# First batch's q and k: rotation products added by accumulating f32 transposes, one v scale, a rewritten order

## The chip, the core and the metric

The kernel runs on one core of a Trainium2 chip. The metric is the device time of one execution in microseconds (us). Five engines work side by side: PE (matrix multiply, with its weight loads, PEld), DVE (vector), ACT (scalar, activation functions), POOL (general) and SP, which here only issues DMAs. Each runs its own list of instructions in order and waits on semaphores for the others.

## What is computed

Attention with rotated q and k over 4 batches, 8 heads, 576 positions and 64 channels, then a feed-forward layer over all 2304 rows:

```python
x1, x2 = x[..., :half], x[..., half:]           # half = 32, x is q or k
rot = concat([x1*cos - x2*sin, x1*sin + x2*cos], -1)
scores = rot_q @ rot_k.T / sqrt(64)
attn = exp(scores - max(scores)); attn = attn / (attn.sum(-1) + 1e-9)
x = attn @ v                                    # to (2304, 512)
h = x @ w_in                                    # w_in 512 x 2048
out = (h * sigmoid(h)) @ w_out                  # w_out 2048 x 512
```

## The kernel before, in words

Heads are taken in pairs p = 0 to 3. A unit u is half a batch (two chunks of 128 rows); what is left of each batch, 64 rows, forms one more unit, "rem". A slot is one head of a pair with one chunk of rows: scores (task `S`), row maximum, exponential, and the transposed probabilities. The feed-forward layer goes by steps (u, i) with i = 0 to 7 over eight pieces of w_in and w_out: `m1` is 24 matmuls (L1200), then tanh, gating and a split into two f16 parts on ACT, DVE and POOL, then two `m2` tasks of 6 matmuls each (L1257). Weights and most operands are split into a high and a low f16 part, which needs a scale: a mean square, spread over the partitions by a matmul with ones, and cut to a power of two by three tiny DVE operations (`add_scale`, L299 to L323, tasks sc0, sc1, sc2).

The first unit is handled apart, since nothing can overlap it yet. Its q and k stay in f32 (`add_qk_first`, L432): the load puts head j and four rows side by side; r0 (L458) writes x, its halves swapped, times sin into a tile `rt`; r1 (L462) multiplies x by cos in place; r2 (L465) adds the two. Each handles 576 columns in one instruction on DVE or POOL. `tr` (L471 to L478) then makes 10 transposes on PE into a PSUM tile, and `ev` copies it to SBUF. The slots of unit 0 (`add_slot_first`) use f32 matmuls (L915) and f32 transposes (L928).

The first batch's v is split as well (`add_v`, L612): a Gram matrix on PE (`trace`, L343) and its diagonal on DVE give the sum of squares of each pair; each pair has its own ones matmul (L647) and its own scale. `add_v_scale` (L690) forms one more scale over the maximum of the four, by a transpose, a maximum and another matmul (L695 to L701).

A raw weight piece is loaded into a place of the weight tiles or of a ring (three parts a, b, c), truncated (wT, wC, wX: L766, L773, L779), its mean square is found by Gram matmuls on PE (L351) or by a Square on ACT (L807), and it is split (whi, wlo). While batch 0 is raw, its q, k and v lie in places that later weights want.

What runs when is written out by hand. `add` records a task with its engines, its dependencies and buffers; the string `ORDER` (L38) lists all 2557 tasks by number, each with its engine (s = SP, t = PE, a = ACT, d = DVE, p = POOL), and the loop at the end of the kernel issues them in this order. An engine's list is thus the order of its letters in the string, and nothing reorders it.

Of the kernel before, what the change touches and what calls it, by code (L numbers as in the profile page):

```python
# [8 lines left out]
F32 = mybir.dt.float32  # L9
# [29 lines left out]
498s 500p 499a 4s 501d 1s 5d 2s 6d 7p 10p 11d 12d 26s 3s 8t 27d 28d 0d 13t 29p 494s 32d 9a 14d 495a 496a 15s 504t 689t  # L39
497d 502a 690d 33p 505d 34p 699t 691a 700d 16t 30t 17d 18t 31a 503d 506t 59s 19d 20d 507d 508d 21d 48s 692t 49p 50d  # L40
509d 81s 60t 704t 51d 514s 61d 62t 63d 64d 701a 702t 82t 693a 54d 512a 510p 511d 83d 22a 52t 65d 513d 703a 53a 35t 36a
55d 66a 84t 85d 516a 694t 24d 695d 696a 37s 38t 39d 86d 70s 76d 518s 56p 520a 71d 87d 68d 515a 88a 705d 40t 706a 57t
72p 519a 41d 697t 698a 42d 90d 707t 709t 522s 523a 58a 521d 524p 92t 525d 528t 25s 517d 526a 77p 527d 93d 540s 708d
529d 541a 73d 710d 43d 78d 44d 94t 530t 531d 532d 99s 533d 711a 46d 74t 75a 538p 101s 102a 103a 539p 1901d 536d 712t
110p 713a 560s 714t 95d 715d 719t 720d 588s 724t 716a 717t 590p 721a 537p 718a 116d 104t 562p 725d 726a 722t 723d 79t
727t 542a 544s 105d 80a 96d 728a 106d 678d 561a 107d 1902t 546a 97d 729t 739t 740d 741a 730d 731a 534p 734t 735d 589a
1903d 736a 535d 1904t 742t 743a 100s 117p 732t 733a 1908d 564s 565a 1905d 591d 545a 737t 738a 563d 47s 749t 750d 751a
744t 1911t 752t 745d 566a 547d 746a 111p 112p 113a 543d 1906p 753a 584s 585a 550t 747t 567d 1907p 118d 548t 551d 568t
549d 569d 580s 570a 571d 552t 553d 119p 748a 132s 554d 586p 572t 555d 558p 587d 581a 582a 573d 754t 755d 756a 759t
760d 1915d 574d 1909t 764t 765d 575d 1910a 761a 1912d 108d 583d 757t 758a 762t 766a 1922d 763a 556p 592a 1916t 594t  # L50
559p 595d 767t 593d 768a 1917d 596t 597d 598d 1923t 769t 557d 785t 69s 578a 599d 770d 602p 604a 1913p 1918t 786d 771a
# [141 lines left out]
def rope_attention_silu_ffn(  # L193
# [99 lines left out]
    th_v = [sm(NPC) for b in range(B)]  # L293
    alpha, alpha_g, c_st = sm(NPC), sm(NPC), sm(NPC)
    r_max, rem_os = sm(1), sm(2)
    bits_r = [sm(2) for _ in range(4)]
    bits_n = [0]

    def add_scale(key, src, inv, s, deps, bufs, it, last=True):  # L299
# [1072 lines left out]
```

## Time and profile before

| | us |
|---|---|
| median of 3 runs | 638.02 (636.32 to 639.64) |
| the profiled execution | 635.93 |
| its span, first to last instruction | 634.1 |
| PE busy in the span | 595.7 (94%) |
| DVE, ACT, POOL busy | 473.4 (75%), 393.1 (62%), 325.4 (51%) |
| mean granted clock of PE, as a share of full speed | 0.976 |

Busy time is the union of an engine's instructions. A row of a timeline gives start, length, engine, line, operation, output and inputs; "idle before" names what ended the wait. The chain of waits is found from the last instruction backwards, at each step to what released it. The granted clock is 1.00 at 2.4 GHz and 0.50 at 1.2 GHz; a window's value is the mean over it.

### The profile page before, as it was taken

To read this page: it belongs to the slowest core of one execution; us is meant where nothing else is said; L and a number is where in the kernel's file an instruction comes from. 1 tells how busy PE (TensorE), PEld (TensorE's weight loads), DVE (VectorE), ACT (ScalarE), POOL (GpSimd) and SP (SyncE) were. 2 spreads that over 40 slices of the span, in tenths; PEclk is the share of its full clock that TensorE was granted. 3 is DMA by queue.
4 is the path that set the end of the run, shared out by engine and by line. 5 is a ranking of instruction groups with operands and counts; after the bars stand their busy time and mean duration, and the time that the engine had idled before them with its cause. 6 is when DMAs were issued, how large, how long until landed. Compare 5 with 4: busy or idle time off the path is not lost.

```text
span 634.1 us, 12527 instructions
## 1 busy us (share of the span) xinstructions
PE 595.7 (94%) x4476; PEld 392.9 (62%) x4476; DVE 473.4 (75%) x1088; ACT 393.1 (62%) x816; POOL 325.4 (51%) x286
## 2 busy tenths in 40 slices
PE   0989887999999999999999999999999999999997
PEld 0657654566566656756666666666666676666663
DVE  2796877899999899978878998988799775322211
ACT  1576867998798776868777677666644633112322
POOL 2448244856566646554766256366754665221231
PEclk9975979989999999999999999999999999999999
DMA  6895506998989998989995897897965746200201
GB/s 177 258 318 212 158 2 156 230 242 173 178 177 176 171 181 158 150 170 172 173 208 122 137 173 150 162 193 141 155 111 96 129 80 124 51 1 1 51 2 33
DMA packets 210670, 91.17 MB, mean 144 GB/s; under 512 B 188464, under 2 KB 194352, under 8 KB 210608
## 3 DMA queue, kind: packets, MB, share of 16 engines
q1 hardware_dynamic: 209840, 89.36, 68.2%
q10 hardware_dynamic: 768, 1.02, 0.7%
q8 instruction: 35, 0.57, 0.4%
q14 instruction: 27, 0.22, 0.1%
HBM read 36.73 MB, written 4.72 MB: 65 GB/s over the span
## 4 chain that ended last, share of the span: by engine, by line
PE 79%; DVE 7%; DMA 6%; ACT 4%; SPq 2%; issue 1%; DVEq 0%; ACTq 0%
PE m L1200 28%; PE m L1257 26%; PE s L1043 7%; PE pv L1145 7%; PE s L915 2%; PE s L1034 2%; DMA Tq<-n 1%; DVE pn L338 1%; PE s L928 1%; PE s L1049 1%; DMA w_in<-in_v_dram 1%; DMA w_out<-in_moe_w_out_dram 1%; PE pv L982 1%; DMA w_out<-in_v_dram 1%; PE s L351 1%
## 5 line engine op out<-in xcount | busy, mean ns | idle before, releaser
L1200 PEld LDWEIGHTS <-w_in 128*128 128x128 f16 x1728 | 168.1, 99 | 33.9 <-issue 3.6
L1200 PE MATMUL m<-xh,w_in 128*128 128x256 f16 x1024 | 179.9, 274 | 0.3 <-DVE g L1216 0.3
L1257 PE MATMUL m<-w_out,gh 128*128 128x512 f16 x576 | 171.6, 379 | 0.0
L1200 PE MATMUL m<-xl,w_in 128*128 128x256 f16 x512 | 140.4, 274 | 0.0
L1077 ACT ACTIVATE e<-s,small 128x576 f32<-128x576 f32 x128 | 97.9, 765 | 62.2 <-DVE s L1059 18.4
L1257 PE MATMUL m<-w_out,gl 128*128 128x512 f16 x288 | 109.2, 379 | 0.2 <-POOL gl L341 0.2
L1216 DVE SCALAR_TENSOR_TENSOR g<-g,m 128x512 f32<-128x512 f32 x72 | 49.1, 682 | 70.0 <-ACT g L1212 39.4
L338 DVE SCALAR_TENSOR_TENSOR pn<-e,small,pn 128x576 f16<-128x576 f32 x94 | 85.9, 918 | 4.2 <-ACT pn L332 3.1
L1257 PEld LDWEIGHTS <-gh 128*128 128x128 f16 x576 | 51.8, 99 | 56.0 <-issue 5.1
L1212 ACT ACTIVATE g<-m,small 128x512 f32<-128x512 f32 x64 | 43.6, 682 | 51.4 <-PE m L1200 44.0
L1043 PE MATMUL s<-Tk,Tq 128*128 128x512 f16 (+1 forms) x384 | 60.8, 286 | 2.1 <-ACT e L1077 2.1
L332 ACT ACTIVATE pn<-e,small 128x576 f16<-128x576 f32 x69 | 52.4, 767 | 12.9 <-DVE small L1091 9.5
L1059 DVE TENSOR_SCALAR_CACHE_REDUCE s<-s,small 128x576 f32<-128x576 f32 x67 | 54.3, 816 | 2.0 <-PE s L1043 1.3
L326 POOL TENSOR_SCALAR g<-g,small 128x512 f32<-128x512 f32 x27 | 21.9, 811 | 64.8 <-ACT gh L332 30.7
L1145 PE MATMUL pv<-pt,vh 128*64 128x320 f16 (+1 forms) x504 | 54.1, 290 | 0.0
L326 POOL TENSOR_SCALAR e<-e,small 128x576 f32<-128x576 f32 x34 | 31.0, 911 | 39.6 <-ACT pn L332 16.9
L1257 PEld LDWEIGHTS <-gl 128*128 128x128 f16 x288 | 28.2, 98 | 34.6 <-POOL gl L341 0.7
L326 POOL TENSOR_SCALAR pn<-e,small 128x576 f16<-128x576 f32 x31 | 26.5, 854 | 41.5 <-DVE small L1091 31.5
L341 POOL TENSOR_TENSOR pn<-e,pn 128x576 f16<-128x576 f32 x34 | 45.4, 1335 | 2.8
L1043 PEld LDWEIGHTS <-Tq 128*128 128x128 f16 x384 | 28.3, 100 | 27.5 <-issue 7.0
L332 ACT ACTIVATE gh<-g,small 128x512 f16<-128x512 f32 x40 | 28.7, 718 | 16.5 <-DVE g L1216 11.9
L338 DVE SCALAR_TENSOR_TENSOR gl<-g,small,gh 128x512 f16<-128x512 f32 x45 | 35.7, 793 | 4.0 <-ACT gh L332 2.7
(212 smaller groups left out, 1057.8 us busy)
## 6 DMA issues: line engine op xcount, KB each, us to landing
w_out<-in_moe_w_out_dram SPq DMA_DIRECT2D x4, 1024.0 KB, 5.7
w_in<-in_moe_w_in_dram SPq DMA_DIRECT2D x4, 1024.0 KB, 6.5
out_dram<-ob SPq DMA_DIRECT2D x28, 128.0 KB, 2.4
io<-in_q_dram SPq DMA_DIRECT2D x12, 288.0 KB, 3.2
io<-in_k_dram SPq DMA_DIRECT2D x12, 288.0 KB, 3.7
io<-in_v_dram SPq DMA_DIRECT2D x12, 288.0 KB, 4.2
io<-in_v_dram SPq DMA_DIRECT2D x13, 256.0 KB, 4.5
ring<-in_moe_w_in_dram SPq DMA_DIRECT2D x3, 1024.0 KB, 5.8
```

The source lines that it names most:

```text
L326: e.tensor_scalar(out=out, in0=in0, scalar1=s1, scalar2=s2, op0=ALU.mult, op1=ALU.bypass if s2 is None else ALU.mult)
L332: act.activation(hi, src, AF.Copy, scale=s)
L338: dve.scalar_tensor_tensor(out=lo, in0=src, scalar=s, in1=hi, op0=ALU.mult, op1=ALU.subtract)
L341: e.tensor_tensor(out=lo, in0=src, in1=hi, op=ALU.subtract)
L1043: pe.matmul(o, tq[:, j, 2 * c:2 * c + 2, :], kt[:, r0:r1, js], start=(n == 0), stop=(n == 1))
L1059: dve.tensor_scalar(out=t, in0=t, scalar1=cc[1], scalar2=None, op0=ALU.mult, op1=ALU.min, accum_out=m_of(1, 2),)
L1077: act.activation(buf("e", i), buf("s", i)[:, 0:S], AF.Exp, bias=m_of(1, 2), scale=-1.0 if fused[i] else cc[0], accum_out=m_of(2, 3),)
L1145: pe.matmul(o[64 * j:64 * j + 64, 0:m], vt[part][:, j, s, :], pt[:, a, j, 0:m], start=(z == 0), stop=(z == len(steps) - 1),)
L1200: pe.matmul(t[:, c, 0:n], w[:, wz, kk, fs], xx[:, kk, 0:n], start=(kk == 0 and x == 0), stop=(kk == KD - 1 and x == 2),)
L1212: act.activation(g[:, :, 0:n], t[:, :, 0:n], AF.Tanh, scale=th_v[units[u][0]][:, i:i + 1])
L1216: dve.scalar_tensor_tensor(out=g, in0=g, scalar=1.0, in1=t, op0=ALU.add, op1=ALU.mult)
L1257: pe.matmul(o, gs[gz][:, c, ts], w[:, wz, c], start=(first and c == 0 and x == 0), stop=(last and c == 1 and x == 2),)
```

## The change

For the first batch's q and k the sum r2 is gone. Each of the two products is now written to a tile of its own, sin into `rt` and cos into a tile `n` (which later batches use too; two buffers), with the two heads of a pair interleaved, so that a product is three instructions (256, 256 and 64 columns) in place of one of 576. x itself is no longer written. The transposes became pairs of matmuls in transpose mode, the cos product first and the sin product second into the same PSUM columns, the second accumulating: 12 for a tile in place of 10. The cos product no longer depends on the sin product.

The first batch's v has one scale for hi and lo of all four pairs: five small matmuls with ones into one PSUM row, one run of sc0, sc1, sc2 over 5 columns. The four ones matmuls and their scales, the transpose, the maximum and its matmul are gone; every `vhi` of batch 0 now depends on the Gram diagonals of all four pairs.

The mean square of a weight may be taken on ACT where the piece came in two loads, too. ORDER is new throughout: 2531 tasks.

```diff
...
-498s 500p 499a 4s 501d 1s 5d 2s 6d 7p 10p 11d 12d 26s 3s 8t 27d 28d 0d 13t 29p 494s 32d 9a 14d 495a 496a 15s 504t 689t
+3s 472s 474p 473a 2s 1s 4s 9p 10p 475d 478a 468s 469a 11t 0d 6d 12d 5p 7t 8a 470d 471d 476a 663t 664d 673t 665a 479d
...
-    bits_r = [sm(2) for _ in range(4)]
+    bits_r = [sm(5) for _ in range(4)]
...
-            def r0(e, x4=x4, nm=nm):
-                eng[e].tensor_tensor(out=buf("rt", 0, p, nm), in0=x4()[:, :, ::-1, :], in1=sin_t, op=ALU.mult)
-
-            def r1(e, x4=x4):
-                cs = cos_t[:, :, None, :].to_broadcast([128, NR, 2, 32])
-                eng[e].tensor_tensor(out=x4(), in0=x4(), in1=cs, op=ALU.mult)
-
-            def r2(e, x4=x4, nm=nm):
-                eng[e].tensor_tensor(out=x4(), in0=x4(), in1=buf("rt", 0, p, nm), op=ALU.add)
-
-            n = add("rope", key + (nm, 0), "dp", r0, [("qld",) + key, ("sin0",)], xb + [rt], it)
-            n = add("rope", key + (nm, 1), "dp", r1, [n, ("cos0",)], xb + [rt], it)
-            n = add("rope", key + (nm, 2), "dp", r2, [n], xb + [rt], it)
-
-            def tr(i=i, nm=nm):
+            def turned(which, nm=nm):
+                if which:
+                    return buf("rt", 0, p, nm).rearrange("p r u d -> p (r u d)")
+                return buf("n", 0, p, nm).rearrange("p r d -> p (r d)").bitcast(F32)
+
+            def product(e, which, x4, tab, turned):
+                o = turned(which)
+                for j in range(2):
+                    dst = o[:, 0:512].rearrange("p (a j u d) -> p j a u d", a=4, j=2, u=2)[:, j]
+                    rs = slice(4 * j, 4 * j + 4)
+                    eng[e].tensor_tensor(out=dst, in0=x4[:, rs], in1=tab[:, rs], op=ALU.mult)
+                dst = o[:, 512:576].rearrange("p (u d) -> p u d", u=2)
+                eng[e].tensor_tensor(out=dst, in0=x4[:, 8], in1=tab[:, 8], op=ALU.mult)
+
+            def r0(e, x4=x4, turned=turned):
+                product(e, 1, x4()[:, :, ::-1, :], sin_t, turned)
+
+            def r1(e, x4=x4, turned=turned):
+                product(e, 0, x4(), cos_t[:, :, None, :].to_broadcast([128, NR, 2, 32]), turned)
+
+            def tr(nm=nm, turned=turned):
                 t = buf(turn[nm], "q", p, nm)
                 for a in range(4):
-                    o = t[:, 128 * a:128 * a + 128]
-                    pe.transpose(o, x()[:, i, a + 3:a + 5, :], id_t)
-                    pe.transpose(o[0:64], x()[:, i, a, :], id_t)
-                pe.transpose(t[:, 512:576], x()[64:128, i, 7:9, :], id_t[64:128, 64:128])
-                pe.transpose(t[0:64, 512:640], x()[:, i, 8, :], id_t)
+                    for z in range(2):
+                        pe.matmul(
+                            t[:, 128 * a:128 * a + 128], turned(z)[:, 128 * a:128 * a + 128], id_t,
+                            is_transpose=True, start=(z == 0), stop=(z == 1),
+                        )
...
+
+            nb = bk("n", 0, p, nm)
+            n = add("rope", key + (nm, 0), "dp", r0, [("qld",) + key, ("sin0",)], xb + [rt], it)
+            y = add("rope", key + (nm, 1), "dp", r1, [("qld",) + key, ("cos0",)], xb + [nb], it)
...
+            n = add("qP", key + (nm,), "t", tr, [n, y, ("ident",)], [nb, rt, sb], it)
             add("qE", key + (nm,), "ad", ev, [n], [sb, bk("T" + nm, 0, p)], it)
...
+            for z in ("inv", "s"):
+                vn[b][z], vn[b][z + "_p"] = vn[b][z + "5"][:, NP:NP + 1], vn[b][z + "5"][:, 0:NP]
...
             y = add("vtr", key, "t", gram, [("vld",) + key], [pb] + fb, it)
-            n = add("vsq", key, "d", diag, [y, ("ident",), ("ones",)], [pb], it)
+            add("vsq", key, "d", diag, [y, ("ident",), ("ones",)], [pb], it)
+            n_sc = ("sc2", "vs", 0)
         else:
             n = add("vsq", key, "a", sq, [("vld",) + key], fb + vb, it)
-        n = add("vmm", key, "t", mm, [n, ("ones",)], [pb], it)
-        n_sc = add_scale(("v",) + key, lambda: ps()[:, 256:257], st["inv"], st["s"], [n], [pb], it)
+            n = add("vmm", key, "t", mm, [n, ("ones",)], [pb], it)
+            n_sc = add_scale(("v",) + key, lambda: ps()[:, 256:257], st["inv"], st["s"], [n], [pb], it)
...
+        def mm_first():
+            o = ps()
+            pe.matmul(o[:, 256:256 + NP], ones, st["ss"], start=True, stop=True)
+            for p in range(NP):
+                o1 = o[:, 256 + NP:257 + NP]
+                pe.matmul(o1, ones, st["ss"][:, p:p + 1], start=(p == 0), stop=(p == NP - 1))
+
+        if b == 0:
+            n = add("vmm", (0,), "t", mm_first, [("vsq", 0, p) for p in range(NP)] + [("ones",)], [pb], it)
+            n = add_scale(("vs", 0), lambda: ps()[:, 256:257 + NP], st["inv5"], st["s5"], [n], [pb], it)
+            add("vs3", (0,), "d", xs, [n], (), it)
+            return
...
-            one = len(halves[nm]) == 1
-
...
-                else:
-                    w2 = raws[i, nm, halves_of[i, nm][0]][0]().bitcast(F32)
-                    act.activation(w2[:, 0::2], w2[:, 1::2], AF.Square, accum_out=wn_of[i][:, 2 * z:2 * z + 1])
+                    return
+                for y, h in enumerate(halves_of[i, nm]):
+                    w2 = raws[i, nm, h][0]().bitcast(F32)
+                    o = wn_of[i][:, 2 * z + y:2 * z + y + 1]
+                    act.activation(w2[:, 0::2], w2[:, 1::2], AF.Square, accum_out=o)
 
             def dg(i=i, nm=nm, diag=diag):
                 if not on_act[i, nm]:
...
-            n = add("wtr", (i, nm), "ta" if one else "t", sq if one else gram, [("wX", i, nm, h) for h in halves[nm]], rb + [bk(w_tag, it)], it)
-            diags.append(add("wtd", (i, nm), "d", dg if one else diag, [n, ("ident",)], [bk(w_tag, it)], it))
+            n = add("wtr", (i, nm), "ta", sq, [("wX", i, nm, h) for h in halves[nm]], rb + [bk(w_tag, it)], it)
+            diags.append(add("wtd", (i, nm), "d", dg, [n, ("ident",)], [bk(w_tag, it)], it))
 
         def mm():
-            pe.matmul(buf(w_tag, it)[:, 256:258], ones, wn[:, 0::2], start=True, stop=True)
+            for z, nm in enumerate(("in", "out")):
+                y = len(halves_of[i, nm]) if on_act[i, nm] else 1
+                for h in range(y):
+                    pe.matmul(
+                        buf(w_tag, it)[:, 256 + z:257 + z], ones, wn[:, 2 * z + h:2 * z + h + 1],
+                        start=(h == 0), stop=(h == y - 1),
+                    )
```

Three places of the new order, each before and then now, as the engine's list has it.

SP, the first loads (in_q and in_k are q and k of one pair; w_in and w_out are the tiles in which they lie raw). Before, from the third load on:

```order
L447 DMA w_in<-in_k_dram 64x64 x2
L414 DMA sin_t<-in_sin_dram 128x256 x2
L416 DMA sin_t<-in_sin_dram 64x64 x2
L414 DMA cos_t<-in_cos_dram 128x128 x2
L416 DMA cos_t<-in_cos_dram 64x32 x2
L442 DMA w_out<-in_q_dram 128x2x256
L447 DMA w_out<-in_q_dram 64x64 x2
L442 DMA w_out<-in_k_dram 128x2x256
L447 DMA w_out<-in_k_dram 64x64 x2
L425 DMA id_t<-in_ident_dram 128x128
L745 DMA w_in<-in_moe_w_in_dram 128x4x512
```

Now, from the first load on:

```order
L423 DMA id_t<-in_ident_dram 128x128
L783 DMA w_out<-in_moe_w_out_dram 128x2x1024
L412 DMA cos_t<-in_cos_dram 128x128 x2
L414 DMA cos_t<-in_cos_dram 64x32 x2
L412 DMA sin_t<-in_sin_dram 128x256 x2
L414 DMA sin_t<-in_sin_dram 64x64 x2
L440 DMA w_in<-in_q_dram 128x2x256
L445 DMA w_in<-in_q_dram 64x64 x2
L440 DMA w_in<-in_k_dram 128x2x256
L445 DMA w_in<-in_k_dram 64x64 x2
L777 DMA w_in<-in_moe_w_in_dram 128x4x512
```

The identity moved from behind the loads of two pairs to the front, the tables went ahead of the first pair, and the second pair went behind the first piece of w_in.

DVE, its first instructions (rt and n hold the products; s, pv and mx are PSUM tiles). Before:

```order
L779 SCALAR_TENSOR_TENSOR w_out<-w_out 128x1024
L458 TENSOR_TENSOR rt<-w_in,sin_t 128x576
L462 TENSOR_TENSOR w_in<-w_in,cos_t 128x576 x2
L465 TENSOR_TENSOR w_in<-w_in,rt 128x576
L458 TENSOR_TENSOR rt<-w_out,sin_t 128x576
L462 TENSOR_TENSOR w_out<-w_out,cos_t 128x576
L1306 MEMSET ones 128x128
```

Now:

```order
L811 SCALAR_TENSOR_TENSOR w_out<-w_out 128x1024
L1344 MEMSET ones 128x128
L465 TENSOR_TENSOR n<-w_in,cos_t 128x4x64 x2
L467 TENSOR_TENSOR n<-w_in,cos_t 128x64
L324 TENSOR_SCALAR Tq<-s_166 128x576
L805 TENSOR_SCALAR w_in<-w_in 128x1024
L811 SCALAR_TENSOR_TENSOR w_in<-w_in 128x1024
L958 TENSOR_REDUCE small<-s 128x1
```

Six products and sums ahead of the first eviction became one product; the three others of the first pair stand on POOL, and wC of the first piece of w_in (L805) came over from ACT.

ACT, around the third to fifth exponentials (e is the exponential of a slot, ring a raw weight piece). Before:

```order
L923 ACTIVATE e,small<-s,small 128x576
L771 ACTIVATE ring<-ring 128x512
L766 ACTIVATE ring<-ring 128x1024
L332 ACTIVATE vh<-io,small 128x2x320
L923 ACTIVATE e,small<-s,small 128x576
L766 ACTIVATE ring<-ring 128x512
L935 ACTIVATE pt<-s 128x5x128
L766 ACTIVATE w_in<-w_in 128x512
L484 ACTIVATE Tq<-s_397 128x576
L807 ACTIVATE ring,small<-ring 128x1024
L766 ACTIVATE w_in<-w_in 128x1024
L923 ACTIVATE e,small<-s,small 128x576
```

Now:

```order
L501 ACTIVATE Tk<-s 128x576
L803 ACTIVATE ring<-ring 128x1024
L501 ACTIVATE Tq<-s_397 128x576
L798 ACTIVATE w_in<-w_in 128x512
L961 ACTIVATE e,small<-s,small 128x576 x2
L973 ACTIVATE pt<-s 128x5x128
L839 ACTIVATE ring,small<-ring 128x1024
L803 ACTIVATE ring<-ring 128x512
L798 ACTIVATE ring<-ring 128x512
L973 ACTIVATE pt<-s 128x5x128
L839 ACTIVATE ring,small<-ring 128x512
L839 ACTIVATE w_in,small<-w_in 128x512
```

The fourth and fifth exponentials now follow each other, the fifth ahead of the Square of the ring piece (L839, before L807) in place of behind it, and two more Squares follow.

## Rows read from the trace of the kernel before

**Rows 1.** Page, part 4: the chain that ended last, shares of the span by engine.
```profile
PE 79%; DVE 7%; DMA 6%; ACT 4%; SPq 2%; issue 1%; DVEq 0%; ACTq 0%
```

**Rows 2.** Windows: bounds, length; PE, PEld, DVE, ACT, POOL busy (count); clock, DMA share, GB/s.
```profile
15.80:40.90 25.10, 20.66 (x139) 15.44 (x139) 20.57 (x48) 17.52 (x28) 13.35 (x9) 0.99 0.84 262
40.90:61.00 20.10, 20.03 (x78) 14.60 (x79) 14.71 (x33) 11.40 (x23) 13.12 (x12) 0.50 0.80 294
61.00:103.70 42.70, 35.37 (x239) 23.72 (x238) 32.37 (x64) 31.91 (x57) 17.59 (x16) 0.92 0.30 95
103.70:140.00 36.30, 33.06 (x222) 21.76 (x221) 31.87 (x74) 33.69 (x63) 24.02 (x16) 0.99 1.02 216
140.00:629.00 489.00, 485.97 (x3804) 317.27 (x3802) 370.38 (x870) 295.48 (x646) 253.30 (x229) 1.00 0.70 130
```

**Rows 3.** Timeline: start, length, engine, line, operation [idle before <- what ended it].
```profile
1.74 1.20 SPq L447 DMA_DIRECT2D w_in<-in_q_dram  x2
...
4.77 1.37 SPq L414 DMA_DIRECT2D sin_t<-in_sin_dram  x2
...
8.85 1.11 SPq L416 DMA_DIRECT2D cos_t<-in_cos_dram  x2
...
13.58 0.58 SPq L425 DMA_DIRECT2D id_t<-in_ident_dram  x1
...
15.84 0.45 PE L475 MATMUL s<-id_t,w_in 128*128 128x128 f32 x1 [15.84 <-DMA id_t<-in_ident_dram]
...
23.50 0.27 PE L475 MATMUL s<-id_t,w_out 128*128 128x128 f32 x1
23.61 0.27 PE L476 MATMUL s<-id_t,w_out 128*64 128x128 f32 x1
...
25.22 0.72 ACT L923 ACTIVATE e<-s,small 128x576 f32<-128x576 f32 x1
...
46.93 0.74 ACT L923 ACTIVATE e<-s,small 128x576 f32<-128x576 f32 x1 [0.56 <-DVE small L319]
...
103.68 0.28 PE L1200 MATMUL m<-xh,w_in 128*128 128x256 f16 x1
```

**Rows 4.** Windows of 2 us: length, PE busy, clock, DMA share, GB/s.
```profile
38.00:40.00 2.00, 0.29 (x3) 1.00 0.99 321
```

**Rows 5.** Groups by form: busy us, mean ns, then idle before (DVE, POOL, PE, ACT).
```profile
L992 DVE TENSOR_TENSOR pn<-mx,pn 128x256 f32<-128x256 f32 x2 | 0.8, 412 | 0.5 <-ACT pn L987 0.5
...
L465 DVE TENSOR_TENSOR w_in<-w_in,rt 128x576 f32<-128x576 f32 x2 | 1.5, 757 | 0.0
...
L465 POOL TENSOR_TENSOR w_out<-w_out,rt 128x576 f32<-128x576 f32 x2 | 3.3, 1673 | 3.2 <-DVE w_out L462 3.1
...
L462 POOL TENSOR_TENSOR io<-io,cos_t 128x576 f32<-128x576 f32 x2 | 3.8, 1884 | 1.4 <-DVE small L319 1.4
...
L1005 POOL TENSOR_TENSOR xl<-pn,xh 128x256 f16<-128x256 f32 x3 | 2.9, 959 | 6.5 <-ACT small L1084 4.8 <-ACT xh L1000 1.6
...
L351 PE MATMUL mx<-w_out 128*128 128x128 bf16 x8 | 1.1, 294 | 0.0
...
L807 ACT ACTIVATE w_out<-w_out 128x1024 f32<-128x1024 f32 x2 | 2.4, 1183 | 0.0
```

**Rows 6.** DMA issues: count, KB each, median us from issue to landing.
```profile
w_out<-in_q_dram SPq DMA_DIRECT2D x2, 16.0 KB, 2.4
```

**Rows 7.** Chain of waits, 32 to 46 us: start, length, what.
```profile
32.84 3.66 DMA ring<-in_moe_w_out_dram
...
40.89 2.71 PE s L915 x6
43.60 0.52 PE pv L695 x2
44.12 1.04 PE mx L351 x8
```

More of the change, by code (lines that the diff above doesn't have):

```diff
@@ L38 @@
 ORDER = """
-498s 500p 499a 4s 501d 1s 5d 2s 6d 7p 10p 11d 12d 26s 3s 8t 27d 28d 0d 13t 29p 494s 32d 9a 14d 495a 496a 15s 504t 689t
[L40 to L48, printed above, removed]
@@ new lines @@
+1488t 2240d 2241a 1489D 1447d 382s 1468p 1490d 399s 1469s 1457d 1448d 1449p 344d 2226d 375d 1952a 1953d 1491a 1492d
+360a 2236t 2242d 1450d 1458a 2245t 1470t 1471d 1482a 1472a 408p 1483a 1451s 1459d 2237t 361t 388s 1493d 362d 363d
+2243t 660d 2244t 1484d 2246a 401a 364d 409p 1473a 2247d 1494a 1515t 365a 2248d 1495d 1497t 1498d 1460s 1516d 1517d
+2252t 1485a 1496s 2249p 1486d 1499a 1500a 1501d 2253a 366d 2250t 1502d 2254d 1487s 1518a 367d 1506t 1519a 390s 414d
+2255d 1520d 1524t 2256d 1954t 358s 1521a 345d 2259t 1474d 1522d 400a 2251t 2257t 1475d 1955a 1476a 1507D 415p 1508a
@@ new lines @@
+1750D 2341a 2342d 2343a 1736d 1737a 2338t 2339t 1974d 662d 1751d 1752a 1753a 1769a 1770a 2344d 2351t 1754d 1803t 1738d
+1739s 2352a 2353d 1740t 1755a 1741d 1742d 1743a 1744a 1745d 1756p 1804d 2354a 2355d 1757s 1771a 1772d 1746p 1747d
+2345t 1805a 2346a 1773d 1806a 1774p 2358t 2348t 1776t 1777d 1807d 1748s 1808d 2359a 1778d 1975t 1779a 2360d 1785t
+1786d 1787d 1976a 1780a 1781d 1758t 1759d 2361p 2362p 1760d 2365t 1761a 1762a 2366a 2349a 1977d 1782p 1763d 1783d
+1788a 1789a 2367d 1821t 2356t 2357t 1775s 1794t 1784s 2363t 1809a 1810d 2368a 1811s 1822D 2372t 1823d 1824a 1795D
@@ new lines @@
+1848t 1790d 2369d 2350s 1825a 1764p 2364t 1791a 1765d 2373a 1766s 2374d 1792p 1796a 1797a 1798d 1799d 2375a 1849D
+1826d 1800a 1801p 1850d 1851a 1852d 2379t 1866t 1812t 1867D 1813d 1868a 1869a 1814d 2347s 1870d 2370t 2376d 2371t
+1978t 1827p 1793s 1802s 1828d 1815a 1871d 1853d 1854p 1855d 2380a 2381d 1979a 1839t 1830t 1831d 1829s 1856s 1816d
+2382a 2377t 2378t 1817d 1818a 1819d 1820s 1872d 2383p 1832a 1833a 1834a 2386t 1835d 1836p 2384t 1873d 1874s 1840d
+2387a 1857t 1837d 1841d 1842a 1980d 2388d 2385t 1843a 1844d 1845p 2393t 2389a 1858d 1859d 1860a 1861a 1862d 1863d
@@ new lines @@
+1846d 1838s 1864p 2390d 2394a 2395d 1847s 1981t 1982a 2391t 2392t 2396a 2397d 1983d 2400t 2401a 2402d 2403p 1865s
+1984t 1985a 1986d 2404p 2398t 2411t 2412a 2413d 2399t 2414a 2415p 2405t 2418t 2406a 2408t 2419a 2420d 2421p 2416t
+2422p 2425t 2409a 2410s 2426a 2427d 2417t 2423t 2432t 2428a 2424t 2429p 2433a 2434d 2430t 2439t 2431t 2435d 2436d
+2440a 2437t 2441d 2442a 2443p 2446t 2447a 2448d 2438t 2110s 2444t 2453t 2449d 2450p 2445t 2454a 2451t 2455d 2456a
+2457p 2460t 2461a 2452t 2462d 2458t 2463d 2471t 2459t 2464p 2465t 2472a 2473d 2466d 2478t 2474p 2468t 2407s 2475d
@@ new lines, in tr @@
+                for z in range(2):
+                    pe.matmul(
+                        t[:, 512:576], turned(z)[64:128, 448:576], id_t[64:128, 64:128],
+                        is_transpose=True, start=(z == 0), stop=(z == 1),
+                    )
+                for z in range(2):
+                    pe.matmul(
+                        t[0:64, 512:640], turned(z)[:, 512:576], id_t, is_transpose=True, start=(z == 0), stop=(z == 1)
+                    )
+            nb = bk("n", 0, p, nm)
```

220 lines of the change are left out of this document (104 added, 116 removed).

## The prediction

> **What bounds the kernel now.** I read the page's chain of waits first: 79% of it lies on PE [rows 1]. Then I cut the span into stages [rows 2]. From 140 to 629 us PE is busy for 485.97 of 489.00 us at a granted clock of 1.00: that stretch is PE work laid end to end, and 3.0 us is all that another order could still take out of it. From the first feed-forward step at 103.68 us [rows 3] to 140 PE idles 3.2 of 36.3 us while ACT is busy for 33.69: PE is full and ACT nearly so. Ahead of that no engine is full all the time. PE's first instruction is at 15.84 us [rows 3]; then it works 20.66 of 25.1 us, 20.03 of 20.1 and 35.37 of 42.7 [rows 2]. The column to see next is the clock: from 40.9 to 61 us it is 0.50, the 1.2 GHz level [rows 2], after PE had worked only 0.29 us between 38 and 40 [rows 4]. So the time is the start of the first feed-forward step plus a stretch that hardly gives. The change acts before that start, on a path of loads, rotations, exponentials and a PE at half clock.
>
> **PE work hardly changes.** Each of eight tiles gets two more transposes, one of 128 columns and one of 64. At full clock transposes of 128 columns stand 0.11 us apart (23.50 and 23.61 us [rows 3]). A tile's two thus cost 0.16 us, eight tiles 1.3. In return 24 Gram matmuls go to ACT; eight take 1.1 us [rows 5], 24 some 3.3. Some ten tiny matmuls of the old v scale go, five come. PE saves some 2 us over the run, part of it in idle time. The accumulation itself could cost: the second transpose of a pair adds to columns that the first has just written. If it waited out the 0.27 us that one lasts in place of 0.11, 48 pairs would cost 7.7 us; if it streams, nothing. I take nothing, because from 140 us on PE runs end to end on groups of accumulating matmuls; the upper end stays with the rivals.
>
> **The first rotations.** Before, PE's first transpose waited for the identity, issued at 13.58 us behind the loads of two pairs [rows 3]. Now the identity goes first (0.58), then one weight piece as before, then the eight table loads, which took from 4.77 to 9.96 us, 5.2 in all, then the first q, whose last pieces were issued from 1.74 to 2.94 [rows 3]. They are now issued by 1.74 + 0.58 + 5.2 + 1.2 = 8.7 us. Such pieces, also without a weight load right ahead, took 2.4 us to land [rows 6]: 11.1. Two products on POOL follow. Three instructions replace one: on DVE 256 columns cost 0.41 us where 576 cost 0.76 [rows 5], so 1.09 ns a column and 0.13 fixed, and a split product costs 1.02. On POOL 576 columns cost 1.67 to 1.88 and 256 cost 0.96 [rows 5]; a split product lies between 1.67 and 0.96 twice with a rest of some 0.4, so 2.3 us, if the split costs at all, and I take 1.6 to 1.7, near the lower rows, because little else runs then. PE starts at 11.1 + 3.2 = 14.3 us in place of 15.84: **−1.5**. The first exponential, at 25.22 us [rows 3], also loses the wC that stood ahead of it on ACT. That second gain I don't count: what follows waits for weight pieces whose bytes are no fewer.
>
> **Sums and products elsewhere.** Eight sums go, four of 0.76 on DVE and four of 1.67 or more on POOL [rows 5]. Of 16 products DVE now has five and POOL 11, where it was 11 and five. DVE loses 11 × 0.76 + 4 × 0.76 − 5 × 1.02 = 6.3 us; POOL goes from 9 × 1.7 = 15.3 to 11 × 1.7 = 18.7. POOL is busy 13.35 of 25.1 us in that stage [rows 2], which hides the 3.4; were that cover gone, they would be added to the rotations of the last pair. A dozen tiny operations of the old v scales go as well, by the fixed 0.13 at least 1.6 us; three conversions (wC) come to DVE, some 2. So about 6 us go from the 68 that DVE works between 15.8 and 103.7 us. The work ran on DVE for 77% of those 88 us, but mostly beside the chain; I count a quarter: **−1.5**, with 0 and the whole 6 as its ends.
>
> The clearest row against the change is POOL's price: the same kind of instruction took 1.67 us at one place and 1.88 at another [rows 5]. The Trainium skill, page "SBUF — State Buffer", section "Who interferes with whom", says that a DVE instruction with two SBUF inputs and a reading GpSimd instruction block each other; by it each of the 11 products would cost up to that difference more, an estimate of 2.3 us in all, under the same cover.
>
> **The half-clock stretch.** From 40.89 us the chain is all PE: six score matmuls (2.71 us), the transpose for the old v maximum (0.52, and as much again behind it) and eight weight Grams (1.04) [rows 7]. Grams and maximum go, −2.1 us at this clock; four transposes for the last pair and five tiny matmuls come, +1.1. Net **−1.0**. And the fifth slot's exponential, at 46.93 us before [rows 3], stood behind this and behind a Square of a weight piece; now it follows the fourth. So of the 2.71 us of scores up to 1.7 can fall into PE's idle time between 38 and 40 us [rows 4], after a ring load that ended at 36.5 us had held ACT [rows 7]. I take the whole, **−1.7**, since the last pair's q and k are now loaded ahead of the ring; zero is the other end.
>
> **What ACT pays.** Four more Squares, two of 1024 columns at 1.18 us [rows 5] and two of 512 at about half: 3.5 us, with a short read after each. The first lies in idle time before 18 us. The others, some 2.6 us, stand in stages where ACT is busy 57% to 75% of the time [rows 2]; two fifths: **+1.0**. After 103.7 us ACT is the fuller engine, so a little of what arrives early is given back: **+0.5**, between nothing and the whole gain.
>
> **The sum.** −1.5 − 1.5 − 1.0 − 1.7 + 1.0 + 0.5 = −4.2. Against the profiled execution, 635.93 us (a span of 634.1 and 1.8 around it), that is 631.7. That execution lies 2.1 us under the median of the three runs, 638.02, and I give the median: 638.0 − 4.2 = **633.8**. A difference of less than 0.5%, 3.2 us, is about what a measurement here can't tell from none.
>
> **Rivals.** *The clock holds.* If the earlier q and k fill PE's gap before 40.9 us, the clock may stay at 1.00. The stretch of 20.1 us then shrinks until DVE, busy 14.71 of it [rows 2], is its bound: 5.4 us more, 628.4. For it: one thin window stands ahead of the fall [rows 4]. Against it: the loads that made the gap carry the same bytes.
>
> *The gain is eaten by shared places.* All four pairs' v now wait, before any hi or lo part, for the pair that loads last; raw places and a load buffer come free later, and the next weights land later. And after 103.7 us ACT has only 2.6 us of idle time to give [rows 2]: if its work was not done earlier, PE idles for what it had gained. Some 3.7 us come back: 637.5. For it: ACT's near-full row. Against it: DVE has less to do before the first step.
>
> *PE stays at half clock longer: slower.* In this stage the change takes real matmuls (Grams) from PE and adds transposes. The half clock lasted 20 us with PE busy all along [rows 2]. But transposes alone got faster early on, 0.45 us long at 15.84 us and 0.27 at 23.50 [rows 3]. The Trainium skill, page "TensorE: Matmul & The Clock Gate", section "Part 4: PE-mode transpose", says that transposes don't count as busy for the gate; by it this stretch would last longer, and the early transposes speak against it. From 61 us PE is busy for 83% of its stage [rows 2], so each further microsecond of PE work at half clock costs about one more. The gain is gone at 4.2 us of such work; with 9 us of it the time is 633.8 + 9 = 642.8. The slow accumulation above, up to 7.7 us, ends near there too.
>
> **Chances.** The sum 0.50, the clock holds 0.18, eaten 0.22, longer half clock 0.10. Of the first, 0.36 lies under 634.8 (faster) and 0.14 above (same). Faster 0.36 + 0.18 = 0.54; same 0.14 + 0.22 = 0.36; slower 0.10. The range goes from the first rival's 628.4, with the runs' own spread of 1.5 below it, to 640, the second rival's 637.5 with the upper ends of the ACT terms: 627 to 640.
>
> **What would show it.** Right: the first transpose near 14 us, the fifth exponential by 41, the first feed-forward step between 98 and 100, and PE idle for no more than 4 us in the 36 us after it. Wrong in a step: a first transpose later than 15 us; transposes more than 0.15 us apart at full clock; a first step at 103 or later. A half-clock stretch much shorter or longer than 20 us decides between the outer rivals; a first step at 99 us with a time above 636 is the eaten gain.

## The result, and the profile after

The changed kernel takes 628.66 us (median of 4 runs, 626.92 to 631.0); the kernel before took 638.74 in the same comparison. The ratio is 0.985 (0.980 to 0.990); in a second comparison it was 0.988 (0.984 to 0.992). The forecast was 633.8 against 638.0, a ratio of 0.993: the time lies inside the range given, but the gain is about twice the forecast, and 0.993 lies outside both intervals.

The profiled execution took 631.0 us, the longest of its four, where that of before, 635.93, lay below all of its comparison. So the two traces stand only 4.9 us apart, and the medians 10.1. That gap is a finding of its own, below. A ratio is one of means and leaves out runs over 1.5% above the fastest of their kernel, which the medians keep: one of the eleven of before in the second comparison, two of the six of grams_back below.

Windows of the changed kernel over its own stages (columns as in [rows 2]):

```profile
13.60:38.00 24.40, 17.68 (x122) 13.84 (x123) 15.43 (x31) 12.18 (x19) 17.53 (x29) 1.00 0.78 238
38.00:58.50 20.50, 20.43 (x79) 15.74 (x79) 12.69 (x26) 13.34 (x28) 5.88 (x6) 0.50 0.60 209
58.50:99.40 40.90, 39.74 (x265) 28.32 (x263) 31.13 (x68) 35.88 (x64) 19.08 (x17) 0.87 0.51 166
99.40:135.70 36.30, 32.80 (x216) 20.89 (x213) 34.16 (x73) 32.90 (x62) 23.07 (x18) 0.95 0.89 213
135.70:624.00 488.30, 484.17 (x3810) 318.00 (x3810) 371.89 (x863) 302.64 (x660) 253.43 (x228) 1.00 0.70 130
```

Against [rows 2]: PE's last stage is the same work (484.17 busy of 488.30). The stage at half clock is still there, 20.5 us long, and comes 3 us earlier. Behind it the clock stands at 0.87 and 0.95, where it was 0.92 and 0.99: by this record the execution spent more time at the low level than that of before and was shorter all the same.

Timeline of the changed kernel at the places of [rows 3] (start, length, engine, line, operation, idle before):

```profile
13.66 0.48 PE L479 MATMUL s<-id_t,n 128*128 128x128 f32 x1 [13.66 <-POOL n L465]
...
19.36 1.57 PE L953 MATMUL s<-Tk,Tq 64*128 64x64 f32 x10 [0.74 <-ACT Tk L501]
...
21.65 0.74 ACT L961 ACTIVATE e<-s,small 128x576 f32<-128x576 f32 x1 [1.06 <-DVE small L958]
...
27.06 0.27 PE L479 MATMUL s<-id_t,n 128*128 128x128 f32 x1
27.17 0.27 PE L479 MATMUL s<-id_t,rt 128*128 128x128 f32 x1
...
36.02 1.12 ACT L798 ACTIVATE ring<-ring 128x1024 f32<-128x1024 f32 x1 [4.92 <-DMA ring<-in_moe_w_in_dram]
...
37.78 0.32 PE L953 MATMUL s<-Tk,Tq 64*128 64x64 f32 x1 [3.32 <-ACT pt L973]
...
43.45 0.74 ACT L961 ACTIVATE e<-s,small 128x576 f32<-128x576 f32 x1 [1.51 <-DVE small L958]
...
99.43 0.28 PE L1238 MATMUL m<-xh,w_in 128*128 128x256 f16 x1
```

The first transpose comes 2.2 us earlier, the first exponential 3.6, the fifth 3.5 and the first feed-forward step 4.25. From there on 631.0 − 99.4 = 531.6 us remain, where 635.93 − 103.68 = 532.25 did: nothing is given back. The rows at 36.02 and 37.78 are the new wait: ACT stands 4.92 us at the truncation of a ring piece, the eviction `pt` is queued behind it, and PE waits 3.32 us for the PSUM place that this eviction frees. Right behind that gap the clock falls.

The record of the clock has a hole at the start. Up to its first change it reads 1.00, also where the rows show the lower level: in the changed kernel the first f32 transposes stand 0.21 us apart, and 0.11 only from 17.5 us on, in the kernel before from 20.1 on.

### The profile page after: what moved, and what is told of

Same layout as the page of the kernel before. It is cut to its first block, busy times and chain, and to the rows that moved or that the text cites. A ratio compares the mean times of both kernels' runs of the same rounds, so it can differ in the third digit from the quotient of the medians.

```text
span 629.2 us, 12529 instructions
## 1 busy us (share of the span) xinstructions
PE 595.4 (95%) x4484; PEld 396.9 (63%) x4484; DVE 468.0 (74%) x1062; ACT 401.2 (64%) x834; POOL 323.5 (51%) x304
## 5 line engine op out<-in xcount | busy, mean ns | idle before, releaser
L336 DVE SCALAR_TENSOR_TENSOR pn<-e,small,pn 128x576 f16<-128x576 f32 x85 | 77.4, 914 | 7.3 <-POOL pn L324 3.6
L324 POOL TENSOR_SCALAR e<-e,small 128x576 f32<-128x576 f32 x43 | 37.5, 872 | 57.5 <-ACT pn L330 25.0
L339 POOL TENSOR_TENSOR pn<-e,pn 128x576 f16<-128x576 f32 x43 | 58.5, 1360 | 3.6
L324 POOL TENSOR_SCALAR pn<-e,small 128x576 f16<-128x576 f32 x40 | 36.6, 914 | 46.2 <-DVE small L1129 31.0
L330 ACT ACTIVATE pn<-e,small 128x576 f16<-128x576 f32 x65 | 49.8, 768 | 16.4 <-DVE small L1129 8.4
L1097 DVE TENSOR_SCALAR_CACHE_REDUCE s<-s,small 128x576 f32<-128x576 f32 x57 | 46.1, 815 | 2.4 <-PE s L1087 1.2
L336 DVE SCALAR_TENSOR_TENSOR gl<-g,small,gh 128x512 f16<-128x512 f32 x50 | 41.1, 823 | 5.6 <-ACT gh L330 3.7
L1104 DVE TENSOR_REDUCE small<-s 128x1 f32<-128x576 f32 x51 | 38.0, 747 | 5.4 <-PE s L1081 4.4
L330 ACT ACTIVATE gh<-g,small 128x512 f16<-128x512 f32 x44 | 31.5, 716 | 14.5 <-DVE g L1254 13.1
```

The source lines that it names most:

```text
L324: e.tensor_scalar(out=out, in0=in0, scalar1=s1, scalar2=s2, op0=ALU.mult, op1=ALU.bypass if s2 is None else ALU.mult)
L330: act.activation(hi, src, AF.Copy, scale=s)
L336: dve.scalar_tensor_tensor(out=lo, in0=src, scalar=s, in1=hi, op0=ALU.mult, op1=ALU.subtract)
L339: e.tensor_tensor(out=lo, in0=src, in1=hi, op=ALU.subtract)
L1097: dve.tensor_scalar(out=t, in0=t, scalar1=cc[1], scalar2=None, op0=ALU.mult, op1=ALU.min, accum_out=m_of(1, 2),)
```

## The experiments

All medians and ratios are against the kernel before, run beside them on the same chip. The fourth column is worked out: each run's time at half clock is 2 × (1 − mean granted clock) × span, and the mean over the runs is given with that of the kernel before beside it. It holds only what the record has. The stretch ahead of the first rise is missing: some 4 us in the profiled executions of before and after, but at least 12 in those of act_order, sum_back, old_loads and order_only, and unknown where there is no profile. The last is the first feed-forward step in the profiled execution.

| kernel | median us | ratio (95%) | us at half clock, kernel / before | first step, us |
|---|---|---|---|---|
| after_again | 628.5 | 0.988 (0.984–0.992) | 24 / 33 | 98.3 |
| act_order | 626.4 | 0.984 (0.980–0.988) | 22 / 33 | 92.9 |
| grams_in_gap | 629.0 | 0.989 (0.985–0.993) | 19 / 33 | 95.1 |
| grams_back | 632.8 | 0.989 (0.983–0.996) | 32 / 33 | 94.3 |
| grams_early | 625.9 | 0.984 (0.979–0.989) | 19 / 34 | 91.8 |
| trans_early | 627.9 | 0.986 (0.980–0.991) | 23 / 34 | 91.3 |
| sum_back | 631.1 | 0.991 (0.988–0.994) | 23 / 34 | 95.7 |
| old_loads | 624.4 | 0.983 (0.978–0.989) | 19 / 34 | 92.1 |
| before_rotation | 644.7 | 1.011 (1.007–1.016) | 46 / 37 | 109.5 |
| four_scales | 629.8 | 0.985 (0.981–0.989) | 29 / 37 | 97.6 |
| order_only | 637.3 | 0.998 (0.995–1.000) | 29 / 37 | 105.1 |
| old_loads_fill | 623.1 | 0.978 (0.973–0.983) | 13 / 37 | 96.3 |

**How large is the gain?** The changed kernel again, unaltered.

> The changed kernel unaltered, timed more often. Theory P (the path: the profiled pair of executions tells the gain, 4.3 us at the first feed-forward step and 4.9 us in all; the rest of the 9.6 us between the medians is the clock of single runs): a ratio to the kernel before of 0.990 to 0.993, 631 to 634 us, and within the runs of either kernel the time rises as the granted clock falls. Theory M (the medians tell it: about 9 us, and the profiled execution was a long one): 0.984 to 0.987, 628 to 630 us, with the changed kernel's granted clocks mostly above those of the kernel before.

Measured: 628.47 in six runs against 635.93 in eleven, 7.5 us. Neither theory holds as put: the time lies in M's range, the ratio, 0.988, between the two. But the clock carries part of it. Over the 11, 15 and 17 runs of the kernel before in the three comparisons the time rises by 0.31, 0.33 and 0.34 us for each recorded microsecond at half clock (straight lines; one run had 17.6 of them and took 631.9, another 44.8 and 642.4). In this comparison the means are 628.4 and 636.7, 8.3 apart, with 24.2 and 32.7 us at half clock. So 8.5 × 0.33 = 2.8 us of the gain go with the clock and 5.5 are left at equal clock. That is a relation between runs, with the hole in the record, not an experiment on the clock; within the six runs of the changed kernel the rise is only 0.18.

**Is the early start worth anything?** Only SP's first loads go back, here as its list has them:

```diff
-id_t, w_out<-moe_w_out, cos_t, sin_t, w_in<-q, w_in<-k, w_in<-moe_w_in, w_in<-v, w_out<-q, w_out<-k
+w_out<-moe_w_out, w_in<-q, w_in<-k, sin_t, cos_t, w_out<-q, w_out<-k, id_t, w_in<-moe_w_in, w_in<-v
```

> The changed kernel with SP's first six loads in the order of the kernel before (weight piece, first q and k, sin, cos, second q and k, identity). The first transpose should come at 15.5 to 16 us in place of 13.7 and the first exponential some 2 us later than 21.7. If what is gained at the start passes through to the end: first feed-forward step 2 us later, time 2 to 2.5 us above the changed kernel. If what follows waits for the weight pieces, as the prediction had it for the gain at the exponential: the delay is gone by the fourth exponential (41 us), and the time is within 1 us.

Measured: 624.44, lower than the changed kernel, with intervals that overlap. The timeline of old_loads:

```profile
15.78 0.45 PE L479 MATMUL s<-id_t,n 128*128 128x128 f32 x1 [15.78 <-DMA id_t<-in_ident_dram]
...
22.10 2.88 PE L953 MATMUL s<-Tk,Tq 64*128 64x64 f32 x10 [0.74 <-ACT Tk L501]
...
25.64 0.74 ACT L961 ACTIVATE e<-s,small 128x576 f32<-128x576 f32 x1 [1.85 <-DVE small L958]
...
39.92 0.74 ACT L961 ACTIVATE e<-s,small 128x576 f32<-128x576 f32 x1
...
41.12 0.74 ACT L961 ACTIVATE e<-s,small 128x576 f32<-128x576 f32 x1 [0.37 <-DVE small L958]
```

The first transpose is 2.1 us later and the first exponential 4.0, and still the fourth and fifth exponentials come earlier (39.92 and 41.12, against 41.10 and 43.45). About half of the delay at the exponential isn't the loads' doing. The first ten scores took 2.88 us here and 1.57 in the changed kernel, and the transposes are still 0.21 us apart at 27.55 us: in this execution PE ran at the 1.2 GHz level for some 12 us at least. Even that cost nothing that can be seen; the execution is the shortest of its five. The ring piece landed 5.6 us after its issue at 28.5, at 34.1; with the changed kernel's loads it landed between 34.4 (act_order) and 36.0. So the head start doesn't bring it sooner. Two windows tell where the head start went, 28 to 39 us, first of the changed kernel:

```profile
28.00:39.00 11.00, 5.95 (x48) 4.87 (x48) 7.15 (x13) 5.50 (x8) 8.52 (x12) 0.96 0.84 270
```

and of old_loads:

```profile
28.00:39.00 11.00, 10.67 (x78) 8.23 (x77) 9.42 (x17) 9.05 (x13) 7.52 (x10) 1.00 0.88 262
...
38.00:58.50 20.50, 17.48 (x103) 13.61 (x104) 17.01 (x32) 15.70 (x32) 12.94 (x13) 0.83 0.78 262
```

PE works 5.95 of these 11 us in the one and 10.67 in the other. Who comes early is done early and waits for the ring; who comes late arrives with it, and its clock is 0.83 from 38 to 58.5 us where it was 0.50. How much of the lateness is the loads' and how much the low level's, this execution can't tell; one with the same loads and an earlier rise is at the end of this section.

**Is the gap what costs?** Three evictions on ACT go ahead of the truncation that waits, here as its list has them:

```diff
 L501 ACTIVATE Tq<-s_347 128x576
+L973 ACTIVATE pt<-s 128x5x128
+L501 ACTIVATE Tk<-s 128x576
+L501 ACTIVATE Tq<-s_395 128x576
 L798 ACTIVATE ring<-ring 128x1024
-L973 ACTIVATE pt<-s 128x5x128
-L501 ACTIVATE Tk<-s 128x576
 L803 ACTIVATE ring<-ring 128x1024
-L501 ACTIVATE Tq<-s_397 128x576
```

> The changed kernel, but on ACT the three PSUM evictions that stood behind the truncation of the ring piece (4.92 us of waiting for its load) now stand ahead of it. PE's gap of 3.32 us ahead of 37.8 us should shrink below 1 us. If PE's idle time in that gap is what the clock falls upon: granted clock 1.00 for most of 38 to 58 us, first feed-forward step at 94 to 96 us in place of 99.4, and 4 to 5 us less than the changed kernel (about 625). If the clock falls anyway: the first step at 97 to 98, 1.5 to 2.5 us less. If the ring load and the weights behind it set the end of this stage: first step at 99, no change.

Measured: 626.39, 2.1 us less than the changed kernel beside it, with intervals that overlap, and a first step at 92.9. Windows of act_order:

```profile
28.00:39.00 11.00, 10.70 (x73) 7.45 (x72) 8.35 (x16) 8.34 (x13) 7.32 (x12) 1.00 0.92 300
...
38.00:58.50 20.50, 18.33 (x89) 14.58 (x88) 15.30 (x28) 14.33 (x31) 10.78 (x11) 0.67 0.68 236
58.50:99.40 40.90, 39.07 (x283) 26.77 (x284) 36.33 (x84) 39.75 (x71) 22.20 (x21) 1.00 0.57 166
```

The gap is gone (10.70 of 11 us), though not by the edit alone: in this execution the first ten scores took 2.88 us, so PE came later, and the ring piece landed at 34.4. The clock fell all the same, between 39 and 40 us, where PE had idled 0.3 us in the 11 before and then waited from 39.25 to 40.36 for an exponential. It rose at 46, fell again from 49 to 56, is 1.00 from 58.5 to 99.4, and fell once more ahead of 125 us. The first step came some 6 us earlier, the time only 2: part of the low clock moved behind the first step.

**Does it matter what fills the gap?** The same gap, filled with work of no use, in three ways:

```diff
-            y = add("vtr", key, "t", gram, [("vld",) + key], [pb] + fb, it)
+            y = add("vtr", key, "t", gram_more, [("vld",) + key], [pb] + fb, it)
...
+                for z in range(9 if p == 1 else 1): gram()
...
+                for z in range(8 if p == 3 else 1): gram()
...
+                for z in range(20 if p == 3 else 0): pe.transpose(ps()[:, 0:128], id_t, id_t)
```

The first (p = 1, its task moved ahead of the scores) is grams_in_gap, the second grams_early, the third trans_early.

> The changed kernel with the Gram matmuls of the second pair's v moved into PE's gap at 35 to 38 us and done nine times over there (the sum is restarted each time, so the result is the same): some 2.6 us of extra PE work, where PE waited. Nothing else moves. If the idle time in the gap is what the clock falls upon: granted clock 1.00 after 38 us, first feed-forward step at 95 to 96, 3 to 4 us less than the changed kernel although PE does more. If not: the clock is 0.50 from about 38 us on as before, the scores behind the gap start up to 0.3 us later, and the time is within 1 us of the changed kernel.

> The changed kernel with the five Gram matmuls of the last pair's v (32.5 us) done eight times over, the sum restarted each time: some 2.3 us of extra bf16 matmuls that fill most of PE's gap ahead of 37.8 us and delay neither the scores behind the gap nor an eviction. If matmul work in the gap is what keeps the clock: the fall comes at 45 us or later in place of 38, first feed-forward step 2 to 4 us earlier than in the profiled runs of the changed kernel (98.3 and 99.4), time 626 to 627. If the clock falls at a place of its own: fall at 38 and 628 to 629 us.

> The same place and the same length as grams_early, but filled with 20 f32 transposes of the identity (0.11 us each, 2.2 us) in place of Grams. If PE being occupied is what counts: the same as grams_early. If transposes do nothing for the clock (the prediction's slower rival rests on that): the clock falls at about 38 us as in the changed kernel, and the time is that of the changed kernel, 628 to 629 us.

Windows 38 to 48 us, of the changed kernel, of grams_in_gap, of grams_early and of trans_early:

```profile
38.00:48.00 10.00, 10.00 (x41) 7.88 (x41) 4.52 (x11) 7.50 (x14) 0.95 (x2) 0.50 0.54 183
```

```profile
38.00:48.00 10.00, 8.09 (x72) 6.55 (x69) 6.36 (x13) 7.36 (x14) 1.28 (x1) 1.00 0.49 175
```

```profile
38.00:48.00 10.00, 7.82 (x58) 6.17 (x59) 8.20 (x16) 9.19 (x19) 4.17 (x7) 1.00 0.53 170
```

```profile
38.00:48.00 10.00, 7.83 (x59) 6.27 (x58) 8.63 (x16) 9.30 (x20) 3.75 (x6) 1.00 0.55 166
```

In all three fillings, one profiled execution each, the fall at 38 is gone; another comes at 48 or 49, behind a gap at 45 to 48 us in which PE idles for some 2 us. Transposes do that as well as bf16 matmuls, and the first steps (91.8, 91.3) are alike. In the median grams_early is 2.5 us below the changed kernel and trans_early 0.6, on another chip and with overlapping intervals, so the runs don't tell these two apart. In both profiles the clock also dipped earlier: in grams_early from 32 to 36 us, behind a gap of 1.7 us, in trans_early from 21 to 27, so what the fill does to it isn't settled by these two. grams_in_gap has no such dip: from its first rise at 18 us the clock is 1.00 up to 48, as was expected if the gap is the cause, and the first step came at 95.1. But its v landed late, so PE still idled 2.62 us ahead of 36.36, the scores behind its Grams started at 39.4 in place of 37.8, and the median gains nothing. Nor does idle time alone decide: here 2.62 us passed without a fall, and act_order fell in a wait of 1.1.

**The arithmetic in the new order.** First the sums, back on the engine of the later product, with products in one instruction (the sum goes into `n`, not into x as in the kernel before, so `n` is still held until the transposes):

```diff
-                        pe.matmul(t[:, 128 * a:128 * a + 128], turned(z)[:, 128 * a:128 * a + 128], id_t, is_transpose=True, ...)
+                    pe.transpose(o, y[:, a + 3:a + 5, :], id_t)
+                    pe.transpose(o[0:64], y[:, a, :], id_t)
...
+                if len(summed) == 2:
+                    eng[e].tensor_tensor(out=turned(0), in0=turned(0), in1=turned(1), op=ALU.add)
```

> The changed kernel with the rotation's two products added again on DVE or POOL (the engine of the later product), products in one instruction of 576 columns, and 10 transposes of the sum for a tile in place of 12 accumulating ones. By the prediction the rotation as such is worth the larger part of 1.5 us at the start and 1.5 us of DVE work, less the split's price: first transpose at 14.5 to 15.5 in place of 13.7, first exponential at 23, time 1.5 to 3 us above the changed kernel. Rival (loads and weight pieces bound this stage, the order did it): within 1 us of the changed kernel. Other rival (the accumulation is most of the gain): 4 us or more above.

Measured: 631.1 and 0.991 against the changed kernel's 0.988: 2 to 2.6 us, as expected, but on another chip and with intervals that overlap, so the size isn't shown. First transpose 15.26, first exponential 25.01, the latter again behind ten scores of 2.88 us. old_loads was as late there and lost nothing. If the sum has a price, it should lie behind the start, in the rotations of the later pairs; no run here isolates that.

The mean squares, back on PE (tasks of the first and second w_out and the seventh w_in):

```diff
-478a ... 502a ... 612a
+478t ... 502t ... 612t
```

> The changed kernel with the mean squares of three weight halves (the first and second w_out, the seventh w_in) back on PE as 24 Gram matmuls and DVE diagonals, off ACT. By the sum of the prediction what the Squares cost ACT (+1.0) and what PE loses with its Grams (part of -1.0) cancel: within 1 us of the changed kernel. Rival: the Grams lengthen the half-clock stretch, where eight cost 1.04 us, and the later ones add to a full PE: 2 to 3 us more than the changed kernel. Other rival: ACT is the tighter engine: 1 to 2 us less.

Measured: six runs in two groups, 625.1 and 626.2 with 16 and 14 us at half clock, and four of 632.6 to 635.8 with 39 to 43. The median, 632.8, is 4 us above the changed kernel; the ratio, 0.989, which lacks the two longest runs, hardly. At equal clock the part is worth nothing that these runs show; whether it makes the long low stretches more frequent, six runs can't tell.

The old scales of v:

```diff
-            n_sc = ("sc2", "vs", 0)
+        n = add("vmm", key, "t", mm, [n, ("ones",)], [pb], it)
+        n_sc = add_scale(("v",) + key, lambda: ps()[:, 256:257], st["inv"], st["s"], [n], [pb], it)
```

> The changed kernel with the first v's old scales: a ones matmul and three tiny DVE operations for each pair, and the joint scale over their maximum (transpose, maximum, matmul) behind them; the hi parts no longer wait for the pair that loads last, but stand where the new order has them. By the prediction's sum the maximum's chain was worth about 1 us at half clock and the tiny operations at least 1.6 us of DVE beside other work: 1 to 2 us above the changed kernel (629.5 to 630.5). If the joint wait costs as much as it saves (the rival of the shared places): within 0.7 us of it.

Measured: 0.985 (629.8 beside 639.0), the same as the changed kernel within the intervals. The one scale gains nothing that can be seen, and its joint wait costs nothing.

**The arithmetic and the order apart.** before_rotation is the kernel before with the change's own edit of `add_qk_first`; order_only the changed kernel with the three edits above together.

> The kernel before with the new rotation alone (interleaved products, sum by accumulating transposes, no sums on DVE or POOL); loads, scales, Grams and the order stay, except five tasks of pairs 2 and 3 and of batch 1 that move by a few places because the tile n is now in use. If the rotation's sum in PSUM is worth what undoing it in the new order cost (2.5 us; 3.1 at equal time on half clock): 633 to 634 us, where the kernel before is at 636.1. If it is worth something only where the new order makes room for it: 635.5 to 637. If it carries most of the whole gain: 630 or less.

> The changed kernel's order and loads with the arithmetic of the kernel before: sums on DVE and POOL, four scales and their maximum, the three mean squares back on PE. If the arithmetic makes the gain and the order only follows it: 635 to 637 us, as the kernel before. If the order makes it: 629 to 631. By the three parts measured or expected singly (2.5 for the sums, 1 to 2 for the scales, 2 for the mean squares) added to the changed kernel's 628.5: 634 to 635.

before_rotation is slower: 644.65, 1.011. That is some 7 us, of which 3 go with its longer time at half clock (46 against 37) by the relation above. Its DVE, timeline:

```profile
18.76 0.42 DVE L466 TENSOR_TENSOR rt<-w_out,sin_t 128x256 f32<-128x256 f32 x1 [6.23 <-PE s L490]
```

With the sum on DVE, `rt` was free once the sum was made. Now both product tiles are held until PE has transposed them, there are two of each, and PE's first transpose waits until 15.82 for the identity. So the second pair's products, which the old order has early on DVE, wait 6.23 us behind the first pair's transposes, and the rest of DVE's list with them. The second exponential comes at 29.71 (26.47 in the trace of before), the first step at 109.45 (103.68). What the five moved tasks add to that wasn't tried.

order_only is at 637.3, 0.998: the order alone gains nothing that can be seen. Undone singly, the three parts cost 2 to 2.6 us (sums), nothing to 4 (mean squares) and nothing (scales); undone together they cost nearly the whole gain of 8 to 10. The full old arithmetic isn't in it, since `n` is still held, and the full new arithmetic in the old order wasn't run. Its window:

```profile
38.00:58.50 20.50, 15.15 (x67) 11.07 (x68) 12.87 (x31) 9.76 (x17) 7.51 (x6) 0.58 0.38 125
```

From 38 to 58.5 us every engine idles for a quarter of the time or more, PE for 5.35 us: nothing is full there, and the engines wait for each other (PE 2.83 us for DVE ahead of 56.09, DVE 2.10 for PE ahead of 46.41). That the order, laid out for other durations, makes these waits is argued, not shown.

**The lowest median.** old_loads, and the gap that it has at 44.8 to 46.7 us filled:

```diff
+            for z in range(17 if i == 1 else 0):
+                pe.transpose(buf(w_tag, it)[:, 0:128], id_t, id_t)
```

> old_loads, and 17 f32 transposes of the identity (1.9 us) in PE's gap of 1.93 us at 44.8 to 46.7 us, into unused columns of the tile that PE writes next. In old_loads the clock fell at 49 us, right after that gap. If idle PE time in the gap is what it falls upon: the fall at 49 is gone or later than 53 us, the time on half clock is lower than the 18.5 us of old_loads on average, and the time is 1 to 2 us less (622.5 to 623.5). If the clock falls wherever some idle time lies within the last stretch: the fall moves and the time stays within 1 us of old_loads (624.4).

Measured: 623.1, 0.978, the lowest here, with 13 us at half clock on average. Its interval doesn't touch the changed kernel's of the second comparison (0.984 to 0.992), on another chip, but it overlaps that of the first (0.980 to 0.990), and from old_loads it can't be told apart. The expectation of where the clock falls failed: at 49 to 53 us it was 1.00, but in the profiled execution (630.4, the longest of its six) it fell at 38 already, where old_loads kept it. In this execution the first ten scores took 1.57 us, not 2.88: PE was early again, waited 1.60 us for the eviction `pt` ahead of 36.70, and the clock fell behind that wait. So the late loads alone don't close the gap of the changed kernel, they shorten it (1.60 in place of 3.32), and at 44.8 us there was no gap left to fill. Two executions of one program need not fall at the same place.

## Why the prediction was right and where it failed

The sign and the place hold: the gain is made ahead of the first feed-forward step, forecast at 98 to 100 and found at 99.4 and 98.3, and PE idles 3.5 us in the 36 us behind it, forecast no more than 4. Most of the terms don't: of the four that made the gain, a run supports only the sums, with intervals that overlap, and the rows the fifth exponential in part. That the time lies in the range owes something to luck, since the lower end, 627, comes from a rival whose mechanism the profile refutes. The size was off, by these steps.

- *The half-clock stretch kept its length in the sum; only a rival let it go.* This is the term that was missing: 2.8 us by the relation between runs, which no experiment isolates. The rival, "the clock holds", gave 628.4, near the result, by a mechanism that the profile refutes: the stretch was 20.5 us again. It isn't held or lost once for all: runs of one kernel spend from 18 to 45 us at the low clock, and the changed kernel some 8 fewer on average, though more in the profiled pair (35 against 30).
- *The start, −1.5: worth nothing.* The first transpose came even earlier than forecast (13.66 against 14.3), and old_loads, which gives it all back, isn't slower. The reason stood in the same paragraph, where the gain at the exponential was left out because the next work waits for weight pieces whose bytes are no fewer. It fits the transposes too: at the next piece ACT waits 4.92 us.
- *Sums and products, −1.5: 2 to 2.6* by sum_back, inside the bounds given; the intervals don't show that a quarter was too small a share. The price of a split product on DVE was too low: the five took 8.2 us where 5 × 1.02 = 5.1 was forecast, 1.03 for the one with little beside it (from 26.84 us) and up to 2.07 beside products on POOL (from 30.19). The accumulation is free: transposes stand 0.11 us apart at 27.06 and 27.17, so the upper end of 7.7 falls away.
- *Grams and maximum gone, −1.0, and Squares on ACT, +1.0:* neither shows at equal clock (four_scales, grams_back).
- *The fifth exponential, −1.7:* it was to come by 41 and came at 43.45, because PE's gap was not filled but moved, to 34.5 to 37.8. With the evictions ahead it comes at 40.18 in the execution profiled, and the first step at 92.9: the mechanism was right and the new order didn't use it.
- *Given back, +0.5:* nothing is; 531.6 us remain where 532.25 did. So the rival of the shared places is out.
- *The longer half clock:* out as well, since the stretch was 20.5 us, as before. It drew on the Trainium skill, page "TensorE: Matmul & The Clock Gate", section "Part 4: PE-mode transpose". By that rule trans_early should have fallen at 38 as the changed kernel did; its row shows 1.00 until 48, which speaks against the rule. So does the changed kernel's start: the transposes go from 0.21 us apart to 0.11 at 17.5 us, after nothing but transposes. In old_loads 24 of them from 15.78 us on brought no such rise, which speaks for it. act_order fell after transposes and f32 scores, but while PE waited, and decides nothing. So it stays open here.

What no term could hold is that the parts aren't additive: the rotation costs 7 us in the old order (3 of them with the clock), the order gains nothing with the arithmetic undone, both together gain 8 to 10. I priced the rotation by its instructions and not by how long its tiles are held.

## What to carry to other kernels

Before counting an earlier start as a gain, look for the first later place where that chain meets a transfer that doesn't move: up to there the gain is only idle time, and idle time of PE can cost clock, as behind the gap at 37.8 us. When an operation is taken over by its consumer, the operands' buffers live longer: price the change by who allocates them next, not only by the instructions saved. And where runs of one kernel differ by their granted clock, compare clocks along with medians, and never one profile with one profile.

## What was not expected of the hardware

- f32 transposes that accumulate into the columns just written follow each other every 0.11 us at full clock, as those that don't.
- The time at half clock differs from run to run of one program (18 to 45 us in the kernel before), at some 0.33 us of time for each recorded one; in the profiled executions its stretches lie at different places even for the same kernel (in the changed one 79 to 89 us in the first profile and 78 to 85 in the second, a third stretch at 127 only in the first).
- The first rise came 3.8 us after PE's first transpose in the changed kernel and not within 11.7 in old_loads (0.21 us between transposes still at 27.55); the record of the clock reads 1.00 throughout.
- The clock fell between 39 and 40 us in act_order, after 11 us in which PE was busy for 10.70, most of it transposes and f32 scores, and at the start of a wait of 1.1 us; it held in trans_early at that place after 10.69 such, and in grams_in_gap across a wait of 2.62. What decided it stays open; no run here isolates it.
